# Plane copies without waits on their own buffer, a buffer choice by age, and a new order for attention plus a token-mixing MLP

## The chip, the cores and the metric

One core of one Trainium2 chip. The time is the device time of one execution in microseconds, as the median of three runs. Profiles and times are of the same program.

## The reference

The input x has 2048 rows of 512. It is normalised by row (`xn`), and the result is the sum of x, of full multi-head attention over `xn` (32 heads of 16), and of a two-layer perceptron that mixes over the 2048 rows.

```python
    def _A_ref(x, wqkv, wo):
        qkv = (x @ wqkv).reshape(B, S, 3, H, Dh) ...
        scores = jnp.einsum("bhqd,bhkd->bhqk", q, k) * scale
        p = _softmax(scores, axis=-1)
        o = jnp.einsum("bhqk,bhkd->bhqd", p, v)
        return o ... @ wo

    def _B_ref(x, w1, b1, w2, b2):
        h = _layernorm(x, axis=-1)
        u = _gelu(jnp.einsum("bsd,sf->bdf", h, w1) + b1)
        y = jnp.einsum("bdf,fs->bds", u, w2) + b2
        return y transposed

    xn = _layernorm(x, axis=-1)
    return x + _A_ref(xn, ...) + _B_ref(xn, ...)
```

The exponentials of the softmax are 32 x 2048 x 2048 values, by far the largest elementwise work.

## The kernel before

**Blocks and groups.** Attention is cut into 32 blocks: four query blocks of 512 rows times eight sets of four heads. A block has 16 groups, one for each tile of 128 keys, so there are 512 groups. In a group each of the four heads has a score tile of 128 keys by 512 queries; TensorE makes it with one matmul of 32 rows (`score_mm`, line 655) into a bank of PSUM.

**Two ways to the exponential.** A group belongs to ScalarE or to VectorE. ScalarE's way takes two score tiles at a time from two banks and writes both exponentials with one instruction (`exp_tile`, line 663, 128 x 1024), two instructions a group, from banks 0 to 3 in turn. VectorE's way builds the bits of the exponential by arithmetic on integers: `dve_first` (line 710) turns one score tile of 128 x 512 into 16-bit integers that are read as bf16, four such first copies a group; they fill a *plane* of 128 x 2048. `add_plane` (line 715) then makes two more planes from it by adding a shift, so that the sum of the three approximates the exponential. VectorE's scores go to banks 4, 5 and 7. Both ways end in TensorE's products with the values (`pv_mm`, line 675), gathered in bank 6: four matmuls for a ScalarE group, four for each plane of a VectorE group. The reciprocal of the softmax's sum and its product follow for each block on VectorE, through memory, and on GpSimd (POOL).

**Planes.** There are 19 places for planes. Two, in `plx`, serve nothing else. The others lie over tensors that are no longer needed at some time: four over `x_sb`, four over `xn_sb`, two each over `h_sb`, `w1blk` and `wqkv_sb`, three over `xnT`. The recording layer knows dependencies by keys, and `plane_alias` holds the keys of the tensor under a plane. `dve_first` and `add_plane` name them among what they write. `plane_take` takes the first free place of the list (`planes_avail`).

**Who decides the order.** Each operation is recorded by `Sched.add` (line 202) with its keys, an occupied interval and a latency. A planner in the kernel keeps a clock for each engine (`pe_step`, `dve_step`, chains of background work), picks the next operation for the engine that is free, and so writes the order of all five engines when the program is built. Which group goes to which engine follows from it as well: `d_take` and `d_fetch` hand a group to VectorE when one of its banks is free. The intervals of VectorE come from `T_DVE` (line 420). The planner's choices are steered by `POLICY`, one row of weights for each 10 us of its clock. `plan` (line 262) turns dependencies into semaphore waits. On the chip each engine runs its own list in that order and waits for semaphores only; TensorE in particular takes scores, value products and all other matmuls in the written order.

**Start and end.** The first four tiles of x are normalised, transposed, and give the first queries and keys, in an order written out by hand; scores begin after it. At the end `tail_epilogue` normalises the last block and adds four row tiles of the output: for the tiles in `HL` the rest of the sum is split in two bf16 parts by POOL and added by identity matmuls (`part_mm`), and ScalarE copies the bank; for the others VectorE adds it.

The two statements around which the change turns:

```python
                          reads=[("bank", bk)], writes=[("pl", pb, r)] + plane_alias[pb], name="p1", **T_DVE(512))
...
            pb = planes_avail()[0]
```

Of the kernel before, what the change touches and what calls it, by code (L numbers as in the profile page):

```python
# [15 lines left out]
D = 512  # L16
# [48 lines left out]
class Op:  # L65
# [26 lines left out]

SEG = 10000.0
POLICY = [
# [245 lines left out]
def bass_parallel_sum__softmax_full_mha__mixer_token_mlp__prompt_kernel(  # L340
# [18 lines left out]
    with ExitStack() as es:  # L359
# [60 lines left out]
        def T_DVE(n, div=1.0):  # L420
            return dict(occ=(n / div + 70.0) / 0.96, lat=(n / div + 70.0) / 0.96 + 135.0)
# [138 lines left out]
        def ln_norm(t):  # L560
            return sc.add("dve", lambda e: e.tensor_scalar(xn_sb[:, t, :], x_sb[:, t, :], mv[:, t, 0:1], mv[:, t, 2:3],
                                                           ALU.subtract, ALU.mult),
                          reads=[("x", t), ("mv", t), ("mvr", t)], writes=[("xn", t)], occ=300, lat=440, two=True)
# [17 lines left out]
        def ln2_norm(t):  # L581
            return sc.add("dve", lambda e: e.tensor_scalar(h_sb[:, t, :], xn_sb[:, t, :], r2[:, t:t + 1], None,
                                                           ALU.mult),
                          reads=[("xn", t), ("r2",)], writes=[("h", t)], occ=300, lat=440, two=True)
# [52 lines left out]
        def v_scale(t0_, n, T):  # L637
# [5 lines left out]
                          writes=[("V", 1, t0_ + i, T) for i in range(n)], two=True, **T_DVE(136 * n, 2.0))  # L643
# [63 lines left out]
        plane_i = [z.bitcast(I16) for z in plane_b]  # L707

        def dve_first(g, r, bk, pb):
            return sc.add("dve", lambda e: e.tensor_scalar(plane_i[pb][:, 512 * r:512 * (r + 1)], bank(bk), BIAS, 0.0,  # L710
                                                           ALU.add, ALU.max),
                          reads=[("bank", bk)], writes=[("pl", pb, r)] + plane_alias[pb], name="p1", **T_DVE(512))

        def add_plane(j, pb0, pb):
# [3 lines left out]
                          writes=[("pl", pb, r) for r in range(4)] + plane_alias[pb], name="plane", two=True, **T_DVE(2048, 4.0))  # L718
# [71 lines left out]
        xnT_evac(1, 1, 5, 0, "act")  # L790
        transpose_mm(2, 0, 0)
# [3 lines left out]
        k_mm(0, KB, 0)  # L795
        transpose_mm(3, 1, 0)
        xnT_evac(3, 1, 1, 0, "dve")
        k_evac(0, 1, KB, 0, "act")
        for t in range(3):
            qt0_mm(t, QB)  # L800
# [3 lines left out]
        k_mm(1, 3, 0)  # L804
        k_mm(2, 3, 1)
        k_mm(3, 3, 2)
# [3 lines left out]
        k_evac(1, 3, 3, 0)  # L810
# [16 lines left out]
        TOL, JOIN, DEFER, P1_PRI, D_PEND, FAR, D_HUNGRY, PACE, N_SAME, PRESS, PL_PRI, D_LAST, SEED = POLICY[0]  # L827
        kt_done = {0: 4}
        vt_done = {0: 4}
        k0_done = set(range(NPRE))  # L830
# [126 lines left out]
        def chain_ut(ft, due, rel):  # L957
# [15 lines left out]
            def u_evac():  # L973
# [3 lines left out]
                    reads=[("bank", xb), ("b1h",)], writes=[("gT", ft)], occ=650, lat=800)  # L977
# [1017 lines left out]
```

## Time and profile before

| | |
|---|---|
| median of three runs | 689.53 us (689.36 to 689.55) |
| profiled execution | 689.35 us, its span 687.1 us |
| granted TensorE clock | 1.00 |
| ScalarE (ACT) busy | 675.5 us, 98% |
| VectorE (DVE) busy | 660.6 us, 96% |
| TensorE (PE) busy | 649.8 us, 95% |
| GpSimd (POOL) busy | 68.3 us, 10% |
| moved from and to memory | 32.65 MB, 48 GB/s on average |

A row of a group reads: line of the kernel, engine, operation, what it writes and reads, shapes, how often; then busy time and the mean duration of one in ns; then the idle time of the engine just before these instructions and what ended it. A row of the timeline reads: start and duration in us, engine, line, operation, and how many equal instructions follow each other in it. `PEld` is TensorE's loading of weights, which overlaps its matmuls.

### The profile page before, as it was taken

To read this page: it belongs to the slowest core of one execution; us is meant where nothing else is said; L and a number is where in the kernel's file an instruction comes from. 1 tells how busy PE (TensorE), PEld (TensorE's weight loads), DVE (VectorE), ACT (ScalarE), POOL (GpSimd) and SP (SyncE) were. 2 spreads that over 40 slices of the span, in tenths; PEclk is the share of its full clock that TensorE was granted. 3 is DMA by queue.
4 is the path that set the end of the run, shared out by engine and by line. 5 is a ranking of instruction groups with operands and counts; after the bars stand their busy time and mean duration, and the time that the engine had idled before them with its cause. 6 is when DMAs were issued, how large, how long until landed. Compare 5 with 4: busy or idle time off the path is not lost.

```text
span 687.1 us, 15560 instructions
## 1 busy us (share of the span) xinstructions
PE 649.8 (95%) x6200; PEld 197.5 (29%) x6287; DVE 660.6 (96%) x1159; ACT 675.5 (98%) x737; POOL 68.3 (10%) x100
## 2 busy tenths in 40 slices
PE   8999999999999999999999999999998999999987
PEld 4433333322222222222222222222222222222222
DVE  7889999999999999999999999999999999999996
ACT  6999999999999999999999999999999999999996
POOL 6610100000000000000000001000000000001110
PEclk9999999999999999999999999999999999999999
DMA  7151100022212222210021211221120212212001
GB/s 215 32 100 26 34 26 4 28 49 46 63 40 53 49 59 48 43 29 18 21 53 48 53 43 43 54 52 37 43 55 23 60 47 62 57 46 62 14 22 46
DMA packets 78367, 32.65 MB, mean 48 GB/s; under 512 B 63004, under 2 KB 74204, under 8 KB 78296
## 3 DMA queue, kind: packets, MB, share of 16 engines
q1 hardware_dynamic: 77864, 31.27, 18.9%
q8 instruction: 49, 0.80, 0.5%
q10 hardware_dynamic: 432, 0.39, 0.2%
q14 instruction: 22, 0.18, 0.1%
HBM read 26.08 MB, written 2.61 MB: 42 GB/s over the span
## 4 chain that ended last, share of the span: by engine, by line
ACT 84%; PE 11%; DVE 3%; issue 1%; DMA 0%; POOL 0%; DVEq 0%
ACT pT L663 84%; PE ps L655 4%; PE ps L675 4%; PE ps L995 1%; DVE x_sb L710 1%; DVE plx L710 1%; PE ps L964 1%; DVE x_sb L715 1%; DVE plx L715 1%; PE ps L1712 0%; DMA x_sb<-in_A_x_dram 0%; PE ps L1005 0%; PE ps L1013 0%; DVE stats L527 0%; PE ps L596 0%
## 5 line engine op out<-in xcount | busy, mean ns | idle before, releaser
L663 ACT ACTIVATE pT<-ps 128x1024 bf16<-128x1024 f32 x720 | 661.0, 1128 | 0.7 <-PE ps L655 0.5
L655 PE MATMUL ps<-QT,KT 32*128 32x512 bf16 x2048 | 288.8, 384 | 23.1 <-ACT pT L663 18.6
L710 DVE TENSOR_SCALAR plx<-ps 128x512 int16<-128x512 f32 x344 | 225.0, 678 | 2.6 <-PE ps L655 1.6
L710 DVE TENSOR_SCALAR x_sb<-ps 128x512 int16<-128x512 f32 x244 | 166.1, 683 | 7.0 <-PE ps L655 0.8
L655 PEld LDWEIGHTS ps<-QT,KT 32*128 32x128 bf16 x2048 | 72.8, 91 | 271.2 <-ACT pT L663 254.5
L675 PE MATMUL ps<-pT,V 128*32 128x512 bf16 x1440 | 143.0, 390 | 0.7 <-DVE V L592 0.4
L715 DVE TENSOR_SCALAR x_sb<-plx 128x2048 int16<-128x2048 int16 x135 | 91.3, 683 | 0.3
L675 PEld LDWEIGHTS ps<-pT,V 128*32 128x32 bf16 x1440 | 36.9, 93 | 80.5 <-issue 73.8
L675 PE MATMUL ps<-plx,V 128*32 128x512 bf16 x592 | 56.9, 382 | 0.5 <-issue 0.5
L675 PE MATMUL ps<-x_sb,V 128*32 128x512 bf16 x592 | 56.3, 382 | 0.0
L1243 POOL TENSOR_TENSOR oT<-OT,denb 128x512 bf16<-128x512 f32 x16 | 20.3, 1270 | 316.0 <-DVE x_sb L715 210.9
L964 PE MATMUL ps<-h_sb,w1blk 128*128 128x512 bf16 (+1 forms) x153 | 49.4, 386 | 2.3 <-issue 2.2
L995 PE MATMUL ps<-gT,w2blk 128*128 128x512 bf16 (+1 forms) x149 | 48.3, 385 | 2.5 <-issue 2.4
L675 PE MATMUL ps<-x_sb,V17b 128*32 128x512 bf16 x484 | 47.5, 383 | 0.8 <-issue 0.3
L1243 POOL TENSOR_TENSOR otmp<-OT,denb 128x512 bf16<-128x512 f32 x15 | 19.1, 1272 | 262.6 <-DMA denb<-rec_scr 109.9
L715 DVE TENSOR_SCALAR x_sb<-x_sb 128x2048 int16<-128x2048 int16 x65 | 44.1, 682 | 0.4 <-PE ps L675 0.4
L715 DVE TENSOR_SCALAR plx<-x_sb 128x2048 int16<-128x2048 int16 x54 | 37.6, 696 | 0.3 <-PE ps L675 0.3
L596 PE MATMUL ps<-xnT,wqkv_sb 128*128 128x512 bf16 (+1 forms) x166 | 34.5, 305 | 2.1 <-issue 1.6
L1206 DVE COPY OT<-ps 128x512 f32<-128x512 f32 x31 | 21.1, 680 | 0.0
L596 PE MATMUL ps<-wqkv_sb,xnT 128*128 128x128 bf16 x256 | 20.9, 221 | 0.0
L995 PEld LDWEIGHTS ps<-gT,w2blk 128*128 128x128 bf16 (+1 forms) x176 | 12.4, 97 | 25.5 <-issue 22.1
L964 PEld LDWEIGHTS ps<-h_sb,w1blk 128*128 128x128 bf16 (+1 forms) x176 | 12.4, 99 | 25.3 <-issue 22.6
(96 smaller groups left out, 335.7 us busy)
## 6 DMA issues: line engine op xcount, KB each, us to landing
denb<-rec_scr SPq DMA_DIRECT2D x124, 64.0 KB, 2.2
w1blk<-in_B_w_dram SPq DMA_DIRECT2D x10, 512.0 KB
w2blk<-in_B_w_dram SPq DMA_DIRECT2D x16, 320.0 KB
xres<-in_A_x_dram SPq DMA_DIRECT2D x16, 128.0 KB, 2.1
QT<-qst SPq DMA_DIRECT2D x120, 16.0 KB, 1.8
out_dram<-osb SPq DMA_DIRECT2D x14, 128.0 KB, 1.7
wqkv_sb<-in_A_wqkv_dram SPq DMA_DIRECT2D x3, 384.0 KB, 8.3
x_sb<-in_A_x_dram SPq DMA_DIRECT2D x2, 512.0 KB
```

Source lines behind the costliest of these rows:

```text
L596: return sc.add("pe", lambda e: e.matmul(dst, lhsT=lhsT, rhs=rhs, start=(ct == 0), stop=(ct == NCT - 1)), reads=reads, writes=[("bank", bk ...
L655: return sc.add("pe", lambda e: e.matmul(bank(bk), lhsT=KT[32 * r:32 * r + 32, T, 128 * kt:128 * (kt + 1)], rhs=QT[32 * r:32 * r + 32, slo ...
L663: return sc.add("act", lambda e: e.activation(pT[:, buf, :], ps[:, slot * 1024:(slot + 1) * 1024], ACTF.Exp, scale=EXP_SCALE), reads=[("ba ...
L675: return sc.add("pe", lambda e: e.matmul(bank(PV_BANK)[32 * r:32 * r + 32, :], lhsT=vt_[:, off:off + 32], rhs=rhs, start=start, stop=stop, ...
L710: return sc.add("dve", lambda e: e.tensor_scalar(plane_i[pb][:, 512 * r:512 * (r + 1)], bank(bk), BIAS, 0.0, ALU.add, ALU.max), reads=[("b ...
L715: return sc.add("dve", lambda e: e.tensor_scalar(plane_i[pb], plane_i[pb0], float(SHIFT[j]), BITS_MAX, ALU.add, ALU.min), reads=[("pl", pb ...
L964: op = sc.add("pe", lambda e: e.matmul(bank(xb)[0:m, :], lhsT=w1blk[:, slot, st, 0:m], rhs=h_sb[:, st, :], start=(st == 0), stop=(st == NT ...
L995: op = sc.add("pe", lambda e: e.matmul(bank(xb), lhsT=w2blk[0:m, slot, ft, :], rhs=gT[0:m, ft, :], start=first, stop=last), reads=([("w2bl ...
L1206: op = sc.add("dve", lambda e: e.tensor_copy(OT32[:, eb, :], bank(PV_BANK)), reads=[("bank", PV_BANK)], writes=[("OT32", eb)], **T_DVE(512))
L1243: op = sc.add("pool", lambda e: e.tensor_tensor(dst, OT32[:, eb, :], denb[:, :], ALU.mult), reads=[("OT32", eb)] + [("denb", r) for r in r ...
```

## The change

It has six parts.

1. `dve_first` and `add_plane` write only the plane's own keys. The last operations on the tensor beneath are looked up once, when a place is first used (`plane_after`), and given as dependencies.
2. `plane_take` takes the free place whose last use ended first by the planner's clock (`plane_free`), in place of the first of the list.
3. Intervals and latencies of VectorE's operations are other numbers: `T_DVE`, both norms, the scaled copy of V, the bias copy, the reciprocal.
4. Keys of tiles 1 to 3 leave the hand-written start and become a chain (`chain_k1`) that the planner places; only tile 0 is there at first. The matmuls of the first queries move up between the transposes.
5. Two first copies of one group whose banks are neighbours may become one instruction (`dve_first2`), where the policy's new last number allows it.
6. `HL` loses the fourth tile, and all rows of `POLICY` are new, with one more number each.

```diff
 POLICY = [
-    (115.0, 80.0, 250.0, -1, 0, 1300.0, 0.0, 0.05, 2, 3, 2, 7500.0, 0),
-    (95.0, 50.0, 250.0, -1, 0, 2000.0, 0.0, 0.0, 3, 3, 2, 10500.0, 63069),
...
+    (115.0, 80.0, 250.0, -1, 0, 1300.0, 0.0, 0.05, 2, 3, 2, 7500.0, 0, 0.0),
+    (210.0, 40.0, 250.0, -1, 0, 900.0, 300.0, 0.05, 3, 2, 2, 7000.0, 0, 1.0),
...
         def T_DVE(n, div=1.0):
-            return dict(occ=(n / div + 70.0) / 0.96, lat=(n / div + 70.0) / 0.96 + 135.0)
+            return dict(occ=(n / div + 64.0) / 0.96, lat=(n / div + 64.0) / 0.96 + 141.0)
...
+        plane_old = {}
+        def plane_after(pb):
+            if pb not in plane_old:
+                z = set()
+                for k in plane_alias[pb]:
+                    z.update([sc.last_writer[k]] if k in sc.last_writer else [])
+                    z.update(sc.readers.get(k, ()))
+                plane_old[pb] = sorted(z, key=lambda o: (o.eng, o.pos))
+            return plane_old[pb]
...
-                          reads=[("bank", bk)], writes=[("pl", pb, r)] + plane_alias[pb], name="p1", **T_DVE(512))
+                          reads=[("bank", bk)], writes=[("pl", pb, r)], extra_deps=plane_after(pb), name="p1", **T_DVE(512))
+        def dve_first2(g, r, bk, r2_, bk2, pb):
+            dst = plane_i[pb].rearrange("p (r n) -> p r n", n=512)[:, r:r2_ + 1:r2_ - r, :]
+            src = ps.rearrange("p (b n) -> p b n", n=512)[:, bk:bk2 + 1:bk2 - bk, :]
+            return sc.add("dve", lambda e: e.tensor_scalar(dst, src, BIAS, 0.0, ALU.add, ALU.max),
+                          reads=[("bank", bk), ("bank", bk2)], writes=[("pl", pb, r), ("pl", pb, r2_)], extra_deps=plane_after(pb),
+                          name="p1", **T_DVE(1024))
...
-                          writes=[("pl", pb, r) for r in range(4)] + plane_alias[pb], name="plane", two=True, **T_DVE(2048, 4.0))
+                          writes=[("pl", pb, r) for r in range(4)], extra_deps=plane_after(pb), name="plane", two=True, **T_DVE(2048, 4.0))
...
         xnT_evac(1, 1, 5, 0, "act")
+        qt0_mm(0, QB)
+        k_mm(0, KB, 0)
         transpose_mm(2, 0, 0)
         ln_norm(3)
         v_ones(0)
         xnT_evac(2, 1, 0, 0, "dve")
-        k_mm(0, KB, 0)
+        qt0_mm(1, QB)
+        k_evac(0, 1, KB, 0, "act")
         transpose_mm(3, 1, 0)
         xnT_evac(3, 1, 1, 0, "dve")
-        k_evac(0, 1, KB, 0, "act")
-        for t in range(3):
-            qt0_mm(t, QB)
+        qt0_mm(2, QB)
         qt0_mm(3, 4)
         qt_evac(0, QB, "act", 0, 384)
         qt_evac(0, 4, "act", 384, 512, "QTh")
-        k_mm(1, 3, 0)
-        k_mm(2, 3, 1)
-        k_mm(3, 3, 2)
...
-        k_evac(1, 3, 3, 0)
...
-        k0_done = set(range(NPRE))
+        k0_done = {0}
...
-        HL = (0, 1, 3)
+        HL = (0, 1)
...
+        def chain_k1(due):
+            def kdone():
+                op = k_evac(1, 3, 5, 0)
+                k0_done.update((1, 2, 3))
+                return op
+            c = Chain("k1", [Step("pe", lambda t=t: k_mm(t, 5, t - 1), 226) for t in (1, 2, 3)]
+                      + [Step("dve", kdone, 470, frees=True)], due, -1.0, bk=[5])
+            c.banks = (5,)
+            return c
...
+        ex_queue.append(chain_k1(-2.0))
         ex_queue.append(chain_v0(-0.95))
...
+        def plane_free(pb):
+            t = sc.ready(writes=[("pl", pb, r) for r in range(4)])
+            return max([t] + [o.end for o in plane_after(pb)]) if pb not in plane_old else t
...
-            pb = planes_avail()[0]
+            pb = min(planes_avail(), key=plane_free)
...
+        def d_pairs(heads, banks):
+            banks = banks[:len(heads)]
+            if PAIR:
+                heads.sort(key=lambda h: (h[0]["g"], h[1]))
+                banks.sort()
+            return list(zip(heads, banks))
...
+                    for k2 in dbank:
+                        if PAIR and k2 == k + 1 and dbank[k2] is not None and dbank[k2][0] <= t + PAIR and dbank[k2][1] is dbank[k][1] \
+                                and dbank[k2][2] > dbank[k][2]:
+                            def p12(k=k, k2=k2):
...
+                                op = dve_first2(dg["g"], r, k, dbank[k2][2], k2, dg["pl"][0])
```

The other new intervals, in ns: norm 300 to 318, second norm 300 to 264, bias copy 650 to 658, reciprocal 175 to 186; the scaled copy of V is planned at four elements a cycle in place of two.

More of the change, by code (lines that the diff above doesn't have):

```diff
@@ L562, in ln_norm @@
                                                            ALU.subtract, ALU.mult),
-                          reads=[("x", t), ("mv", t), ("mvr", t)], writes=[("xn", t)], occ=300, lat=440, two=True)
+                          reads=[("x", t), ("mv", t), ("mvr", t)], writes=[("xn", t)], occ=318, lat=450, two=True)
         def ln2_rs(i):
@@ L583, in ln2_norm @@
                                                            ALU.mult),
-                          reads=[("xn", t), ("r2",)], writes=[("h", t)], occ=300, lat=440, two=True)
+                          reads=[("xn", t), ("r2",)], writes=[("h", t)], occ=264, lat=405, two=True)
         ps_bf = ps.bitcast(BF16)
@@ L642, in v_scale @@
                           reads=[("V", 0, t0_ + i, T) for i in range(n)] + [("Vone", t0_ // 4)],
-                          writes=[("V", 1, t0_ + i, T) for i in range(n)], two=True, **T_DVE(136 * n, 2.0))
+                          writes=[("V", 1, t0_ + i, T) for i in range(n)], two=True, **T_DVE(136 * n, 4.0))
         def blk_of(g):
@@ L826, in bass_parallel_sum__softmax_full_mha__mixer_token_mlp__prompt_kernel @@
         pv_open = [True]
-        TOL, JOIN, DEFER, P1_PRI, D_PEND, FAR, D_HUNGRY, PACE, N_SAME, PRESS, PL_PRI, D_LAST, SEED = POLICY[0]
+        TOL, JOIN, DEFER, P1_PRI, D_PEND, FAR, D_HUNGRY, PACE, N_SAME, PRESS, PL_PRI, D_LAST, SEED, PAIR = POLICY[0]
         kt_done = {0: 4}
         vt_done = {0: 4}
-        k0_done = set(range(NPRE))
+        k0_done = {0}
         v0_done = set()
@@ L976, in u_evac @@
                     gT[0:m, ft, :], bank(xb)[0:m, :], b1h[0:m, ft:ft + 1], None, ALU.add),
-                    reads=[("bank", xb), ("b1h",)], writes=[("gT", ft)], occ=650, lat=800)
+                    reads=[("bank", xb), ("b1h",)], writes=[("gT", ft)], occ=658, lat=800)
                 ut_done[0] += 1
@@ L1221, in rec @@
                 return sc.add("dve", lambda e: e.reciprocal(den_s[:, eb, :], den_s[:, eb, :]),
-                              reads=[("den_s", eb)], writes=[("den_s", eb)], occ=175, lat=330)
+                              reads=[("den_s", eb)], writes=[("den_s", eb)], occ=186, lat=330)
             def out1():
@@ L1663, in pe_step @@
                             frb.sort(key=lambda k: sc.ready(writes=[("bank", k)]))
-                            heads = list(zip(d_take(len(frb), p), frb))
+                            heads = d_pairs(d_take(len(frb), p), frb)
                         score_mm(g, p[0], 2 * slot, False)
@@ L1687, in pe_step @@
                 frb = [q for q in d_room() if sc.ready(writes=[("bank", q)]) <= t]
-                hs = list(zip(d_take(len(frb)), frb))
+                hs = d_pairs(d_take(len(frb)), frb)
                 if hs:
@@ L1782, in dve_step @@
                     c.append((P1_PRI if all(dbank[q] or ex_active[q] for q in dbank) else 1, dbank[k][0], p1))
+                    for k2 in dbank:
+                        if PAIR and k2 == k + 1 and dbank[k2] is not None and dbank[k2][0] <= t + PAIR and dbank[k2][1] is dbank[k][1] \
+                                and dbank[k2][2] > dbank[k][2]:
+                            def p12(k=k, k2=k2):
+                                _, dg, r = dbank[k]
+                                op = dve_first2(dg["g"], r, k, dbank[k2][2], k2, dg["pl"][0])
+                                dbank[k] = dbank[k2] = None
+                                dg["n1"] += 2
+                                dg["t"] = max(dg["t"], op.end)
+                                if dg["n1"] == 4:
+                                    pv_items[dg["g"] // NKT].append((dg["t"], "D", dg["g"], dg["pl"][0], 0))
+                            c.append((c[-1][0], c[-1][1] - 1e-3, p12))
             pool_on = sc.wide > t
@@ L1838, in bass_parallel_sum__softmax_full_mha__mixer_token_mlp__prompt_kernel @@
             while n_seg[0] * SEG <= t:
-                TOL, JOIN, DEFER, P1_PRI, D_PEND, FAR, D_HUNGRY, PACE, N_SAME, PRESS, PL_PRI, D_LAST, SEED = POLICY[min(n_seg[0], len(POLICY) - 1)]
+                TOL, JOIN, DEFER, P1_PRI, D_PEND, FAR, D_HUNGRY, PACE, N_SAME, PRESS, PL_PRI, D_LAST, SEED, PAIR = POLICY[min(n_seg[0], len(POLICY) - 1)]
                 n_seg[0] += 1
```

132 rows, old and new, of the table POLICY are left out of this document.

## The prediction

> **What bounds the kernel now.** I read the page first (busy shares, then the chain of waits), then the groups by line for ScalarE (ACT) and VectorE (DVE).
>
> ```profile
> span 687.1 us, 15560 instructions
> PE 649.8 (95%) x6200; PEld 197.5 (29%) x6287; DVE 660.6 (96%) x1159; ACT 675.5 (98%) x737; POOL 68.3 (10%) x100
> ACT 84%; PE 11%; DVE 3%; issue 1%; DMA 0%; POOL 0%; DVEq 0%
> ...
> L663 ACT ACTIVATE pT<-ps 128x1024 bf16<-128x1024 f32 x720 | 661.0, 1128 | 0.7 <-PE ps L655 0.5
> ...
> L710 DVE TENSOR_SCALAR plx<-ps 128x512 int16<-128x512 f32 x344 | 225.0, 678 | 2.6 <-PE ps L655 1.6
> L710 DVE TENSOR_SCALAR x_sb<-ps 128x512 int16<-128x512 f32 x244 | 166.1, 683 | 7.0 <-PE ps L655 0.8 <-PE ps L675 0.5
> ```
>
> ACT is on the chain for 84% of the span, and one line of it, the exponential, is 661.0 us in 720 instructions with 0.7 us of idle time before them all. 661.0 / 720 = 0.918 us is what one more or one less is worth (the mean of 1128 ns is longer, because neighbours overlap). The ACT rows in order of time give the rest of the skeleton:
>
> ```profile
> 9.08 1.57 ACT L616 ACTIVATE QT<-ps,qmask 128x384 bf16<-128x384 f32 x4 [0.68 <-PE ps L596]
> 10.52 20.38 ACT L663 ACTIVATE pT<-ps 128x1024 bf16<-128x1024 f32 x22
> ...
> 669.60 10.19 ACT L663 ACTIVATE pT<-ps 128x1024 bf16<-128x1024 f32 x11
> 682.51 1.09 ACT L590 ACTIVATE osb<-ps 128x512 bf16<-128x512 f32 x2 [2.72 <-PE ps L1013]
> 684.02 0.60 ACT L590 ACTIVATE xres<-ps 128x512 bf16<-128x512 f32 x1 [0.42 <-PE ps L1013]
> ```
>
> The first exponential starts at 10.52, the last ends at 669.60 + 10.19 = 679.79, and 7.3 us of closing work follow. So the time is 10.5 us of start, a full ACT, and 7.3 us of tail. The 96% of DVE matters too: it is the second engine that is nearly full, and what ACT no longer does has to be done there.
>
> **The change, term by term.** *Exponentials.* The policy table steers an order written when the program is built, so I counted the instructions of both built programs. Exponentials: 720 before, 714 after. Groups of four heads given to DVE: 152 before, 155 after. The sum has 6 x 0.918 = 5.5 us less on ACT. It is worth that only if scores arrive in time, which is DVE's side of the account.
>
> *DVE's new work.* Three groups are 12 more first copies (L710) and 6 more plane copies (L715). What does one occupy?
>
> ```profile
> 301.35 0.68 DVE L715 TENSOR_SCALAR x_sb<-plx 128x2048 int16<-128x2048 int16 x1
> 301.95 1.48 DVE L710 TENSOR_SCALAR x_sb<-ps 128x512 int16<-128x512 f32 x2
> ...
> 312.26 1.28 DVE L710 TENSOR_SCALAR x_sb<-ps 128x512 int16<-128x512 f32 x2
> ...
> 318.45 1.28 DVE L710 TENSOR_SCALAR plx<-ps 128x512 int16<-128x512 f32 x2
> 319.65 0.68 DVE L715 TENSOR_SCALAR x_sb<-x_sb 128x2048 int16<-128x2048 int16 x1
> 320.25 0.68 DVE L710 TENSOR_SCALAR plx<-ps 128x512 int16<-128x512 f32 x1
> ```
>
> Start to start it is 0.60 us for either kind (301.35 to 301.95, 319.65 to 320.25); the 0.68 contains the overlap with the next one. So 18 x 0.60 = 10.8 us more. Twelve of the copies are issued as six double ones over two banks. No row shows such an instruction; one lies between 0.60 (one copy) and 1.20 (two copies). I take 1.20, because its elements are those of two; the other end would give back 3.6 us.
>
> *The false waits.* Of the pairs above, the one at 301.95 takes 1.48 us, so its second copy starts 1.48 - 0.68 = 0.80 after the first; the two at 312.26 and 318.45 start 0.60 apart. In the DVE stream, 301.95 is two copies into one plane of x_sb, 312.26 two planes of x_sb, 318.45 one plane of plx. Only planes laid over another tensor (x_sb, xn_sb and others) carry that tensor's keys, and two writers of the same keys wait for each other; plx has none. The stream has 57 such neighbours in x_sb and 7 in xn_sb: 64 x 0.20 = 12.8 us of DVE time that the change frees. In the changed stream 153 neighbours fall on one aliased plane, none with such a wait.
>
> The Trainium skill speaks against this term: "VectorE: DVE Perf Modes", section "The DRAIN you can't avoid", has eight copies taking 13.88 us with a semaphore after each and with one after the last, so that the semaphore costs nothing. By it the change would free nothing here; the trace disagrees (0.80 against 0.60), and the measurement decides. What follows if the 0.20 is not the wait's is a rival below.
>
> *Does DVE keep up?* Busy time by stretch, columns PE, PEld, DVE, ACT, POOL:
>
> ```profile
> 36.00:200.00 164.00, 158.30 (x1550) 51.33 (x1573) 158.96 (x283) 163.46 (x179) 9.85 (x8) 1.00 0.20 43
> 200.00:330.00 130.00, 124.61 (x1180) 34.80 (x1194) 127.47 (x215) 129.86 (x142) 8.90 (x7) 1.00 0.18 40
> 330.00:500.00 170.00, 160.05 (x1497) 45.06 (x1519) 167.03 (x282) 169.98 (x183) 10.16 (x8) 1.00 0.18 45
> 500.00:670.00 170.00, 160.02 (x1552) 44.84 (x1569) 166.80 (x281) 170.00 (x187) 15.41 (x14) 1.00 0.18 45
> ```
>
> DVE's idle time from 36 to 670 us is 5.04 + 2.53 + 2.97 + 3.20 = 13.7 us. A false wait shows only 0.80 - 0.68 = 0.12 of its 0.20 as idle; the other 0.08 x 64 = 5.1 us are inside "busy". So DVE has 18.8 us above its bare work: 12.8 false waits and 6.0 other. The change asks 10.8 for new work and 5.5 because the span shrinks: 16.3, which leaves 2.5 us in that stretch. If all 6.0 us of other idle time are waits that DVE cannot shed, ACT is held for 6.0 - 2.5 = 3.5 us; if it is slack, for nothing. A second count goes along the two streams, from the first DVE copy to the last (each tied by its bank to the score and so to a number of exponentials): at 0.60 a copy, DVE lies 23 us below ACT's time before and about 5 after, and from the 200th exponential on the two run level. That is a close fit, with some room at its two ends, so I take +1.5 us, between 0 and 3.5.
>
> *Start.* Keys of tiles 1 to 3 now come after the first scores, and their copy to KT stands in the DVE stream behind four instructions that it used to precede:
>
> ```profile
> 8.75 0.68 DVE L527 BATCH_NORM_STATS2 stats<-x_sb 128x6 f32<-128x512 bf16 x1
> 9.46 0.18 DVE L531 BATCH_NORM_AGGREGATE mv<-stats 128x2 f32<-128x6 f32 x1
> 9.99 0.56 DVE L592 CAST KT<-ps 128x384 bf16<-128x384 f32 x1 [0.35 <-PE ps L596]
> 10.47 0.68 DVE L527 BATCH_NORM_STATS2 stats<-x_sb 128x6 f32<-128x512 bf16 x1
> 11.19 0.18 DVE L531 BATCH_NORM_AGGREGATE mv<-stats 128x2 f32<-128x6 f32 x1
> 11.29 0.38 DVE L561 TENSOR_SCALAR xn_sb<-x_sb,mv 128x512 bf16<-128x512 bf16 x1
> 11.58 0.69 DVE L527 BATCH_NORM_STATS2 stats<-x_sb 128x6 f32<-128x512 bf16 x1
> ...
> 8.21 1.75 PE L596 MATMUL ps<-xnT,wqkv_sb 128*128 128x128 bf16 x28
> 9.97 0.39 PE L655 MATMUL ps<-QT,KT 32*128 32x512 bf16 x2
> ```
>
> The first scores hang on the four QT copies of ACT, which start when the third tile of QT is through, so the 12 key matmuls taken from behind it (12 of the 28, 12/28 x 1.75 = 0.75 us of PE) free nothing: the first exponential stays at about 10.5. But only one key tile is there, which feeds two exponentials. Without the copy at 9.99 the four instructions move up by its 10.47 - 9.99 = 0.48, the last ending at 11.58 + 0.69 - 0.48 = 11.8; then the copy (0.56) and the scores, which lead their exponential by 10.52 - 9.97 = 0.55: about 12.9 for the third, where an unbroken ACT would want it at 10.52 + 2 x 0.918 = 12.36. I take +0.5, between 0 (the copy finds an earlier place) and 1.0 (all moves are late as well).
>
> *Tail.* The fourth row tile of the end goes through DVE, not ACT, and two identity matmuls and two POOL splits vanish.
>
> ```profile
> 682.52 0.38 PE L1005 MATMUL ps<-wo_c,oT 128*128 128x512 bf16 x1
> 682.74 0.59 PE L1043 MATMUL ps<-gT,ident 128*128 128x512 bf16 x2
> 683.17 0.38 PE L1013 MATMUL ps<-wo_pad,oT 128*128 128x512 bf16 x1
> 683.39 0.59 PE L1013 MATMUL ps<-wo_pad,otmp 128*128 128x512 bf16 x2
> 683.80 0.69 DVE L1905 TENSOR_TENSOR xres<-ps,h_sb 128x512 bf16<-128x512 f32 x1 [1.45 <-PE ps L1013]
> ```
>
> The four matmuls ahead of 683.39 are gone or stand before the wait for otmp, so those at 683.39 can start at 682.52, 0.87 earlier. DVE then adds the third tile at 682.93 and the fourth 0.60 later, ending at 684.22; ACT's copy of it ended at 684.02 + 0.60 = 684.62. So -0.4 (0 if the order before them costs it). The store behind keeps its length.
>
> *At nothing:* the corrected intervals and "longest free first" emit no instruction; they act through the counts above. Three more groups on DVE mean nine more PE batches of plane products and three fewer of pT; PE's weight loads before scores idle mostly for ACT, so six batches are hidden there.
>
> **Sum.** The profiled execution took 689.35, 2.25 more than its span and 0.18 less than the median of 689.53. 689.35 - 5.5 + 1.5 + 0.5 - 0.4 = 685.45; with the 0.18, 685.6.
>
> **Rivals.** (1) *DVE keeps up wholly and the start closes its hole:* 689.53 - 5.5 - 0.4 = 683.6. For it: ACT lost only 0.7 us so far; against: DVE's room fell to 2.5 us. (2) *DVE becomes the bound, and it is slower than before.* Place: from the 200th exponential on, where the two run level. First copies wait for their scores (plx, which has no false waits, idled 2.6 us over 344 copies, 8 ns each). Each wait that the tighter order adds now goes to the end. Break-even is where DVE's unshed time is above what it has by what the change gains: 2.5 us of room plus 5.5 - 0.1 of gain, 7.9 us, or 13 ns for each of 620 copies over today's idle share; at 25 ns, 15.5 - 2.5 = 13.0, and 689.53 - 5.4 + 13.0 = 697.1. Against: the 0.60 us grid holds through the quoted rows. (3) *The 0.20 us is not the wait's.* Then 153 neighbours cost 0.20 each, 30.6 us against the 2.5 us of room, so 28.1 on the path: 689.53 - 5.4 + 28.1 = 712. The row at 312.26 speaks against it: same tensor, no wait, 0.60. This is what the Trainium skill's rule would come to. (4) *The planner's order does not deliver:* ACT loses in many small gaps what six exponentials give: 688.2 to 690.9, no change.
>
> **How the numbers follow.** What a measurement of this kernel can tell from no change is about 0.2%, 1.4 us. Chances: forecast, with its own range 684.4 to 688.0, 0.63; (1) 0.19; (4) 0.08; (2) 0.08; (3) 0.02. Faster 0.82, same 0.08, slower 0.10. The range: low, rival (1) with 0.3 us of it for the double copies, 683.3; high, +3.5 for DVE and +1.0 for the start with no gain in the tail, 689.53 - 5.5 + 4.5 = 688.5.
>
> **What would show it.** Right: 714 exponentials at 0.918 each; neighbours in one plane 0.60 apart and no pair at 0.80; DVE idle under 6 us between 36 and 670; the third exponential about 0.5 us late; last ACT copies two, with two DVE additions behind each other. Wrong: more than 3 us of idle time before the exponentials, with scores held by DVE (rival 2), or pairs still 0.80 apart (rival 3).

## The result, and the profile after

| | before | after |
|---|---|---|
| median | 689.46 us (689.36 to 689.55, 4 runs) | 684.00 us (683.83 to 684.57, 4 runs) |
| profiled execution, its span | 689.35, 687.1 | 684.02, 682.2 |
| exponentials on ACT | 720 | 714 |

The ratio (of the means) is 0.9922, with an interval of 0.9905 to 0.9939: 5.5 us less, where 3.9 us were forecast. The measured 684.0 lies inside the whole range of the prediction (683.3 to 688.5), but outside the narrower range of its forecast (684.4 to 688.0), on the side of the first rival. In the runs below, those with a mean granted clock of 0.991 to 0.993 (two of `e4`, two of `e5`, one of `e9`) came 3 to 4 us above the other runs of their kernel, which hardly moves a median but moves a ratio. First the page of the changed kernel: busy shares, the chain that ended last, and the groups that answer to those of before.

```profile
span 682.2 us, 15375 instructions
PE 645.9 (95%) x6217; PEld 196.9 (29%) x6304; DVE 663.2 (97%) x1172; ACT 669.7 (98%) x730; POOL 66.6 (10%) x98
...
ACT 85%; PE 10%; DVE 3%; POOL 1%; issue 0%; DVEq 0%
...
L664 ACT ACTIVATE pT<-ps 128x1024 bf16<-128x1024 f32 x714 | 655.9, 1135 | 1.1 <-PE ps L656 0.9
...
L722 DVE TENSOR_SCALAR x_sb<-ps 128x512 int16<-128x512 f32 x184 | 120.3, 678 | 0.4
L722 DVE TENSOR_SCALAR xn_sb<-ps 128x512 int16<-128x512 f32 x132 | 86.9, 679 | 2.6 <-PE ps L656 2.2
...
L722 DVE TENSOR_SCALAR plx<-ps 128x512 int16<-128x512 f32 x86 | 56.3, 678 | 0.4 <-PE ps L656 0.4
```

ACT still makes up 85% of the chain, so it still sets the end. Its exponentials are busy for 655.9 us in place of 661.0. Their idle time went from 0.7 to 1.1 us. DVE's copies into `x_sb` lost their idle time (7.0 us for 244 before, 0.4 us for 184 now), though by the built programs 153 neighbours of DVE's list, and no longer 64, now write one aliased plane.

Next the timeline of ACT (start and duration in us; in brackets the idle time before and what ended it).

```profile
9.16 1.57 ACT L617 ACTIVATE QT<-ps,qmask 128x384 bf16<-128x384 f32 x4 [0.86 <-PE ps L597]
10.60 1.95 ACT L664 ACTIVATE pT<-ps 128x1024 bf16<-128x1024 f32 x2
13.18 30.39 ACT L664 ACTIVATE pT<-ps 128x1024 bf16<-128x1024 f32 x33 [0.63 <-PE ps L656]
43.84 18.64 ACT L664 ACTIVATE pT<-ps 128x1024 bf16<-128x1024 f32 x20 [0.28 <-PE ps L656]
...
662.98 12.18 ACT L664 ACTIVATE pT<-ps 128x1024 bf16<-128x1024 f32 x13
678.01 1.08 ACT L591 ACTIVATE osb<-ps 128x512 bf16<-128x512 f32 x2 [2.86 <-PE ps L1030]
```

The first exponential starts at 10.60 (10.52 before), the third after a hole of 0.63. The last one ends at 662.98 + 12.18 = 675.16 (679.79 before), and 682.2 - 675.16 = 7.04 us follow (7.31 before). So the span of 4.9 us less is made of: exponentials -5.1, idle time before them +0.4, first start +0.1, tail -0.3. What lies outside the span was 1.8 us against 2.2.

The 36th exponential starts at 43.84, after 2 + 33 others. In the kernel before it is this one:

```profile
42.82 1.03 ACT L663 ACTIVATE pT<-ps 128x1024 bf16<-128x1024 f32 x1
```

So by then the changed kernel is 1.0 us behind. Its idle time shows 0.63 + 0.28 = 0.9 of it, the first start 0.1. From there to the end of the last exponential it takes 675.16 - 43.84 = 631.3 us for 679, the kernel before 679.79 - 42.82 = 637.0 us for 685. That is 0.930 us each in both.

The timeline of DVE shows the pieces that were forecast from other rows:

```profile
12.15 0.54 DVE L593 CAST KT<-ps 128x384 bf16<-128x384 f32 x1
...
162.58 1.22 DVE L730 TENSOR_SCALAR xnT<-ps 128x1024 int16<-128x1024 f32 x1
163.72 0.68 DVE L735 TENSOR_SCALAR xn_sb<-x_sb 128x2048 int16<-128x2048 int16 x1
...
663.05 2.47 DVE L722 TENSOR_SCALAR wqkv_sb<-ps 128x512 int16<-128x512 f32 x4
...
671.06 0.69 DVE L735 TENSOR_SCALAR x_sb<-plx 128x2048 int16<-128x2048 int16 x1
675.78 0.78 DVE L1927 STREAM_TRANSPOSE denb<-ps 128x256 f32<-128x256 f32 x2 [4.04 <-PE ps L676]
...
678.45 1.29 DVE L1957 TENSOR_TENSOR xres<-ps,h_sb 128x512 bf16<-128x512 f32 x2 [0.59 <-PE ps L1030]
```

The key copy comes at 12.15 and makes the hole. A double copy takes 163.72 - 162.58 = 1.14 us start to start. Four copies into one aliased plane take 2.47 us, that is (2.47 - 0.68) / 3 = 0.60 each, with no wait left between them. DVE is through with its last plane at 671.06 + 0.69 = 671.75, 3.4 us before the last exponential ends. In the kernel before, the same view shows how close that was:

```profile
678.36 0.69 DVE L715 TENSOR_SCALAR x_sb<-plx 128x2048 int16<-128x2048 int16 x1
680.28 0.78 DVE L1875 STREAM_TRANSPOSE denb<-ps 128x256 f32<-128x256 f32 x2 [1.23 <-PE ps L675]
```

There the last plane ended at 679.05, 0.7 us ahead of ACT. So DVE, with three more groups to do, stands 2.7 us further ahead at the end. Busy time by stretch, columns as in the table of before (PE, PEld, DVE, ACT, POOL, granted clock, share of DMA, GB/s):

```profile
36.00:200.00 164.00, 158.73 (x1575) 51.41 (x1592) 159.82 (x288) 163.71 (x180) 9.84 (x8) 1.00 0.20 43
200.00:330.00 130.00, 126.19 (x1206) 35.62 (x1208) 129.84 (x219) 129.92 (x143) 8.66 (x7) 1.00 0.18 41
330.00:500.00 170.00, 160.09 (x1524) 44.98 (x1547) 169.64 (x289) 169.96 (x182) 10.41 (x9) 1.00 0.19 47
500.00:670.00 170.00, 160.48 (x1555) 45.20 (x1575) 169.11 (x287) 169.96 (x186) 13.68 (x12) 1.00 0.18 44
```

DVE's idle time from 36 to 670 us is 4.18 + 0.16 + 0.36 + 0.89 = 5.6 us, from 13.7. From 200 us on it is 1.4 us in 470: both engines are full.

### The profile page after: what moved, and what is told of

Its sections match the earlier page's. It is cut to its first block, busy times and chain, and to the rows that moved or that the text cites. A ratio compares the mean times of both kernels' runs of the same rounds, so it can differ in the third digit from the quotient of the medians.

```text
span 682.2 us, 15375 instructions
## 1 busy us (share of the span) xinstructions
PE 645.9 (95%) x6217; PEld 196.9 (29%) x6304; DVE 663.2 (97%) x1172; ACT 669.7 (98%) x730; POOL 66.6 (10%) x98
## 4 chain that ended last, share of the span: by engine, by line
ACT 85%; PE 10%; DVE 3%; POOL 1%; issue 0%; DVEq 0%
ACT pT L664 84%; PE ps L656 4%; PE ps L676 3%; PE ps L597 1%; PE ps L1012 1%; ACT gT L1003 1%; PE ps L794 1%; DVE stats L528 0%; PE ps L981 0%; POOL r L579 0%; PE ps L749 0%; DVE h_sb L583 0%; DVE xnT L593 0%; DVE xn_sb L562 0%; DVE KT L593 0%
## 5 line engine op out<-in xcount | busy, mean ns | idle before, releaser
L664 ACT ACTIVATE pT<-ps 128x1024 bf16<-128x1024 f32 x714 | 655.9, 1135 | 1.1 <-PE ps L656 0.9
L722 DVE TENSOR_SCALAR x_sb<-ps 128x512 int16<-128x512 f32 x184 | 120.3, 678 | 0.4
L722 DVE TENSOR_SCALAR xn_sb<-ps 128x512 int16<-128x512 f32 x132 | 86.9, 679 | 2.6 <-PE ps L656 2.2
L722 DVE TENSOR_SCALAR plx<-ps 128x512 int16<-128x512 f32 x86 | 56.3, 678 | 0.4 <-PE ps L656 0.4
L722 DVE TENSOR_SCALAR xnT<-ps 128x512 int16<-128x512 f32 x66 | 43.2, 679 | 0.0
L722 DVE TENSOR_SCALAR wqkv_sb<-ps 128x512 int16<-128x512 f32 x56 | 36.7, 679 | 0.2
L676 PE MATMUL ps<-x_sb,V 128*32 128x512 bf16 x344 | 33.3, 381 | 0.0
L676 PE MATMUL ps<-xn_sb,V 128*32 128x512 bf16 x296 | 28.9, 381 | 0.0
L722 DVE TENSOR_SCALAR h_sb<-ps 128x512 int16<-128x512 f32 x44 | 28.8, 679 | 0.0
L722 DVE TENSOR_SCALAR w1blk<-ps 128x512 int16<-128x512 f32 x40 | 26.4, 677 | 0.0
L735 DVE TENSOR_SCALAR xn_sb<-x_sb 128x2048 int16<-128x2048 int16 x31 | 20.9, 680 | 0.0
```

What stands on the lines that cost most here:

```text
L664: return sc.add("act", lambda e: e.activation(pT[:, buf, :], ps[:, slot * 1024:(slot + 1) * 1024], ACTF.Exp, scale=EXP_SCALE), reads=[("ba ...
L676: return sc.add("pe", lambda e: e.matmul(bank(PV_BANK)[32 * r:32 * r + 32, :], lhsT=vt_[:, off:off + 32], rhs=rhs, start=start, stop=stop, ...
L735: return sc.add("dve", lambda e: e.tensor_scalar(plane_i[pb], plane_i[pb0], float(SHIFT[j]), BITS_MAX, ALU.add, ALU.min), reads=[("pl", pb ...
```

## The experiments

In all kernels but two (`e7` and `e8`, which the planner orders anew) the order of every engine's instructions is that of the kernel they start from, apart from what their diff adds or swaps. So a difference comes from the one edit, not from another plan. Each kernel is compared with runs of the kernel before that were made beside it on the same chip: 689.64 us for `e1` to `e4`, 689.84 for `e5` to `e8`, 689.69 for `e9` to `e11`, which ran on another chip. "Dose" means small fills of a scratch tile put into DVE's list; they compute nothing that is used.

### Waits alone

**`e1_before_nowait`**: the kernel before, in its own order, without the waits between two writers of an aliased plane. The planner's clock still sees them; the program doesn't.

```diff
+        own = set()
         for k in writes:
             w = self.last_writer.get(k)
             if w is not None:
-                deps.add(w)
+                if name in ("p1", "plane") and k[0] != "pl" and w.name in ("p1", "plane"):
+                    own.add(w)
+                else:
+                    deps.add(w)
...
-        for d in op.deps:
+        for d in op.deps + list(own):
             t = max(t, d.end)
```

> The kernel before, every engine's order as it was, only the waits between two copies into one aliased plane buffer left out. My account (ACT sets the end, the false waits cost DVE room and not time): 689.4, within 0.5 us of the kernel before, neighbours in one x_sb plane 0.60 us apart in place of 0.80, DVE's idle time between 36 and 670 us up from 13.7 by nothing or more. Rival a (the waits were on the path, so that their removal alone is the gain): 689.5 - 5.5 = 684. Rival b (the 0.20 us belongs to the place and not to the wait): 689.4 and neighbours still 0.80 apart.

Measured: 688.88 us in 12 runs, ratio 0.9988 (0.9979 to 0.9997): 0.8 us less. DVE's timeline, the group of exponentials and the sum of the four stretches from 36 to 670 us:

```profile
301.18 1.28 DVE L714 TENSOR_SCALAR x_sb<-ps 128x512 int16<-128x512 f32 x2
```

```profile
L667 ACT ACTIVATE pT<-ps 128x1024 bf16<-128x1024 f32 x720 | 660.9, 1131 | 0.1
```

```profile
sum 634.00, PE 619.45 PEld 175.66 DVE 619.97 ACT 633.87 POOL 44.43; mean PE 154.86 PEld 43.91 DVE 154.99 ACT 158.47 POOL 11.11
```

The neighbours in `x_sb` of which the prediction showed 1.48 now take 1.28, so they are 0.60 apart, and the 0.20 us was the wait's. In the whole trace 57 pairs of successive copies into `x_sb` or `xn_sb` start 0.77 to 0.82 apart in the kernel before, and 3 in `e1`. But DVE's idle time stays at 634.0 - 620.0 = 14.0 us (13.7 before): the time that 64 waits had taken is now spent waiting for TensorE, for scores above all: 5.9 us of the idle time end with them, from 2.4. ACT's idle time before exponentials fell from 0.7 to 0.1, about what the end moved. The waits filled room; they hardly set the time.

**`e2_after_waits`**: the changed kernel, in its order, with the waits put back between successive writers of one aliased plane.

```diff
+        def same(pb, op):
+            if plane_alias[pb]:
+                if pb in plane_last:
+                    same_buf.append((op, plane_last[pb]))
+                plane_last[pb] = op
+            return op
...
+        for op, d in same_buf:
+            op.deps.append(d)
         sc.plan()
```

> The changed kernel, every engine's order as it is, with the waits between two writers of one aliased plane buffer put back. My account: 153 neighbouring copies at 0.80 us in place of 0.60 cost DVE 30.6 us; its room in this order is some 3 to 6 us, so the time is 684.0 + 25 to 28 = 709 to 712. Rival a (a wait on the engine's own last instruction costs nothing): 684.0. Rival b (half of them fall where DVE would wait for scores anyway): 684.0 + 10 to 15 = 694 to 699.

Measured: 712.71 us in 4 runs, ratio 1.0331 (1.0315 to 1.0348), just above the 709 to 712 that were expected. The changed kernel took 683.89 beside it, so this one is 28.8 us longer. From its page the span, the clock in 40 slices, the chain and the exponentials:

```profile
span 710.7 us, 15834 instructions
...
PEclk9999999999999999999799999999999999999999
...
PE 56%; DVE 33%; issue 5%; ACT 5%; POOL 1%; DMA 0%; DVEq 0%
...
L664 ACT ACTIVATE pT<-ps 128x1024 bf16<-128x1024 f32 x714 | 670.4, 1046 | 15.0 <-PE ps L656 10.1
```

From DVE's timeline:

```profile
299.94 1.48 DVE L730 TENSOR_SCALAR xnT<-ps 128x512 int16<-128x512 f32 x2
301.33 0.68 DVE L743 TENSOR_SCALAR x_sb<-xn_sb 128x2048 int16<-128x2048 int16 x1
301.93 1.48 DVE L730 TENSOR_SCALAR xnT<-ps 128x512 int16<-128x512 f32 x2
```

Pairs are 1.48 - 0.68 = 0.80 us apart again: in the whole trace 145 of successive copies into one aliased tensor are 0.77 to 0.82 apart, against 3 in the changed kernel. ACT's share of the chain falls from 85% to 5%: DVE is late with the banks, TensorE waits in its written order, and ACT behind it. A wait for the instruction just before, on the same engine, is not free here: 153 neighbours at 0.20 are 30.6 us, and the end is 28.8 us later. Not all of that need be the waits'. The granted clock fell to 0.7 in one slice, and its mean was 0.992 to 0.995 in the four runs, where the four runs of the changed kernel in the table above had 0.999 or 1.000. What share the slower clock had was not separated. An estimate from the runs at 0.991 to 0.993 of other kernels is 3 to 4 us, which would leave about 25 for the waits. It may be more here, since TensorE stands on more of this chain.

**`e3_after_again`** is the changed kernel, run beside `e1`, `e2` and `e4`.

> The changed kernel once more, beside the others on the same chip: 684.0 within 0.6 us, span 682, 714 exponentials, first at 10.6, third at 13.2.

Measured: 683.89 us in 6 runs, ratio 0.9914 (0.9900 to 0.9928).

### The hole at the start

**`e4_after_key_copy_first`**: one swap in DVE's list, the key copy of tiles 1 to 3 ahead of the row statistics that stand before it.

```diff
+        ds = sc.streams["dve"]
+        i = ds.index(k1_op[0])
+        late = ds[i - 1]
+        ds[i - 1], ds[i] = ds[i], ds[i - 1]
```

> The changed kernel with one swap on DVE: the copy of the keys of tiles 1 to 3 goes ahead of the row statistics that stand before it. The statistics took 0.59 us start to start. My account: the third exponential comes 0.5 to 0.6 us earlier (12.6 in place of 13.18), ACT is unbroken after it, and the whole run ends 0.5 us earlier: 683.5. Rival (DVE runs level with ACT, so what ACT gains at the start it gives back at the first place where DVE is late): third exponential at 12.6 but the end unchanged, 684.0, with 0.5 us more idle time before the exponentials later on.

Measured: 684.21 us in 6 runs, ratio 0.9932 (0.9912 to 0.9953): no gain. ACT's timeline of `e4`, then that of `e3`:

```profile
10.50 3.94 ACT L664 ACTIVATE pT<-ps 128x1024 bf16<-128x1024 f32 x4
14.67 28.86 ACT L664 ACTIVATE pT<-ps 128x1024 bf16<-128x1024 f32 x31 [0.23 <-PE ps L656]
43.82 16.79 ACT L664 ACTIVATE pT<-ps 128x1024 bf16<-128x1024 f32 x18 [0.29 <-PE ps L656]
```

```profile
10.48 1.95 ACT L664 ACTIVATE pT<-ps 128x1024 bf16<-128x1024 f32 x2
13.07 30.44 ACT L664 ACTIVATE pT<-ps 128x1024 bf16<-128x1024 f32 x33 [0.64 <-PE ps L656]
43.80 16.80 ACT L664 ACTIVATE pT<-ps 128x1024 bf16<-128x1024 f32 x18 [0.28 <-PE ps L656]
```

The swap does close the hole: the third exponential follows the second without a break. Yet both kernels have done 35 exponentials at 43.8 us. By the single starts in the two traces, `e4` is 0.58 us ahead of `e3` at the third exponential, 0.23 at the fifth, and 0.02 behind from the tenth on. The row at 14.67 is the fifth, which waits. What stands before it in `e4` (`PEld` is TensorE's loading of weights):

```profile
13.12 0.40 DVE L562 TENSOR_SCALAR xn_sb<-x_sb,mv 128x512 bf16<-128x512 bf16 x1
...
13.58 0.23 PEld L749 LDWEIGHTS ps<-ident,xn_sb 128*128 128x128 bf16 x4 [0.32 <-DVE xn_sb L562]
...
14.24 0.39 PE L656 MATMUL ps<-QT,KT 32*128 32x512 bf16 x2
```

The same normalisation in `e3`:

```profile
13.11 0.40 DVE L562 TENSOR_SCALAR xn_sb<-x_sb,mv 128x512 bf16<-128x512 bf16 x1
```

DVE normalises a later tile, TensorE waits for it with that tile's transposes (L749), and the fifth exponential's scores (14.24) stand behind them in TensorE's order. DVE's work of the start is the same in both kernels, so this normalisation comes at the same time in both, with or without the hole. That it holds the fifth exponential in `e4` is read from these rows. For the 0.23 us that go between the fifth and the tenth it is argued by likeness, and no run took the normalisation away. That the hole itself doesn't set the time is shown.

### How much room DVE has

**`e5_after_dose`** and **`e6_before_nowait_dose`**: 60 fills, spread over DVE's list from the 130th first copy to the 600th, in the changed kernel and in `e1`.

```diff
+        pad = sb("pad", [128, 128], F32)
+        p1s = [o for o in sc.streams["dve"] if o.name == "p1"]
+        for i in range(60):
+            at = p1s[130 + (600 - 130) * i // 60]
+            x_ = Op("dve", lambda e: e.memset(pad[:], 0.0), "pad")
+            sc.streams["dve"].insert(sc.streams["dve"].index(at) + 1, x_)
```

> The changed kernel, every engine's order as it is, with 60 small fills of a scratch tile (128 x 128 f32, estimated at 0.15 us each, 9 us together) spread over DVE's stream between its 130th and 600th first copy. Account from e4 (DVE runs level with ACT, no room): the time rises by nearly all of it, 683.9 + 7 to 9 = 691 to 693. The prediction's account (2.5 us of room in that stretch): 683.9 + 6.5 = 690.4. Rival (ACT alone sets the end): 683.9.

> The kernel before without the false waits, order as it was, with the same 60 fills. DVE has 13.7 us of visible idle time there, so my account is no change to the same kernel without fills: 688.9, at most +0.7. Rival (the order of 720 exponentials is as tight on DVE as that of 714): 688.9 + 7 to 9 = 697.

Measured: `e5` 685.50 us in 10 runs, ratio 0.9945 (0.9928 to 0.9961), 1.6 more than the changed kernel (2.1 by the two ratios, which go by means); `e6` 689.20 in 10 runs, ratio 0.9995 (0.9985 to 1.0005), 0.3 more than `e1`. DVE's timeline of `e5` gives the true dose:

```profile
306.29 0.68 DVE L722 TENSOR_SCALAR x_sb<-ps 128x512 int16<-128x512 f32 x1
306.94 0.17 DVE L1997 MEMSET pad<- 128x128 f32 x1
307.03 0.62 DVE L722 TENSOR_SCALAR x_sb<-ps 128x512 int16<-128x512 f32 x1
307.57 0.67 DVE L735 TENSOR_SCALAR xn_sb<-xn_sb 128x2048 int16<-128x2048 int16 x1
```

Two copies and a fill take 307.57 - 306.29 = 1.28 us where two copies take 1.20. A fill of 0.17 us thus costs only 0.08, and the dose is 60 x 0.08 = 4.8 us, about half of what the expectation reckoned. Both accounts in it (690.4, and 691 to 693) were too high; with the true dose, the prediction's 2.5 us of room would give 686.2. Of 4.8 us, 1.6 to 2.1 reach the end and about 3 are swallowed. DVE's share of the chain rises to 62%, ACT's falls to 19%:

```profile
DVE 62%; ACT 19%; PE 15%; issue 1%; DMA 1%; POOL 1%; SPq 1%; DVEq 0%
```

So the changed kernel has some 3 us of room on DVE and no more. The order of before, once its waits are out, takes the same dose for 0.3 us.

**`e9_after_big_dose`**, **`e10_before_big_dose`**, **`e11_before_nowait_big_dose`**: 180 fills over the same stretch of the list (14.4 us by the 0.08 above), in the changed kernel, in the kernel before with its waits, and in `e1` without them. Each fill follows the one before by a wait as well.

```diff
+        for i in range(180):
+            at = p1s[130 + (600 - 130) * i // 180]
+            x_ = Op("dve", lambda e: e.memset(pad[:], 0.0), "pad")
+            x_.deps = [last_pad] if i else []
+            last_pad = x_
```

> The changed kernel, order as it is, with 180 of the small fills between DVE's 130th and 600th first copy. In e5 a fill made the distance of its neighbours 1.28 us in place of 1.20, 0.08 net, so 60 of them were 4.8 us, and the time rose by 1.6: 3.2 us of room. My account: 180 x 0.08 = 14.4 us, less 3.2: 683.9 + 11.2 = 695.1, between 694 and 696.5. Rival (the fills fall mostly into gaps that no account has seen; the rise goes on at a third of the dose): 688.7.

> The kernel before, with its false waits, order as it was, and the same 180 fills. The prediction's account: of its 18.8 us above bare work 12.8 are false waits, which stay, so 6.0 us of room: 689.6 + 14.4 - 6.0 = 698.0, between 696 and 700. Rival (a false wait's 0.20 us can be filled by a fill that comes to stand in it, so the waits are no loss of room): 689.6 to 691.

> The kernel before without the false waits, order as it was, and the same 180 fills. The prediction's account: 18.8 us of room, more than 14.4: 689.2, at most +1.5. Rival (the waits' time was no room that other work can use): the same as with the waits, 696 to 700.

The two values of `e1` and `e3` come from the first chip.

| | without fills | with 180 fills | more | ratio to before |
|---|---|---|---|---|
| changed kernel (`e3`, `e9`) | 683.89 | 694.15 | 10.3 | 1.0077 (1.0049 to 1.0105) |
| kernel before (`e10`) | 689.69 | 697.34 | 7.7 | 1.0112 (1.0097 to 1.0127) |
| the same without waits (`e1`, `e11`) | 688.88 | 690.61 | 1.7 | 1.0016 (1.0006 to 1.0025) |

The chain of `e9`, then of `e10`, then of `e11`:

```profile
DVE 66%; ACT 18%; PE 13%; issue 1%; POOL 1%; DVEq 0%
```

```profile
ACT 40%; PE 31%; DVE 25%; issue 3%; POOL 0%; DMA 0%; DVEq 0%
```

```profile
ACT 69%; DVE 17%; PE 12%; issue 1%; SPq 1%; DMA 1%; POOL 0%
```

Rows two and three are the same order under the same fills, and differ by the waits only: 697.34 - 690.61 = 6.7 us. The rival, that a fill can stand in a wait at no cost, holds for a few of them: 24 fills of `e10` fell between two copies into one aliased tensor, and 20 of these pairs are 0.78 to 0.80 apart, as they are without a fill. That makes its dose some 1.6 us smaller, so the 6.7 us are rather too little. So the waits' time, which was worth 0.8 us by itself (`e1`), is room that other work can use. `e11` rose by 1.7 us, so in that order too the room is used up at some places before the whole 14.4 us are in: DVE has 17% of its chain. `e9` gives the room of the changed kernel a second time, 14.4 - 10.3 = 4.1 us.

### Code and policy apart

**`e7_after_old_policy`**: all code of the change, with the rows of `POLICY` of before and no double copies. **`e8_before_new_policy`**: the code of before with the new rows, without their last number. The first two rows of the one and of the other:

```diff
 POLICY = [
     (115.0, 80.0, 250.0, -1, 0, 1300.0, 0.0, 0.05, 2, 3, 2, 7500.0, 0, 0.0),
-    (210.0, 40.0, 250.0, -1, 0, 900.0, 300.0, 0.05, 3, 2, 2, 7000.0, 0, 1.0),
+    (95.0, 50.0, 250.0, -1, 0, 2000.0, 0.0, 0.0, 3, 3, 2, 10500.0, 63069, 0.0),
```

```diff
 POLICY = [
     (115.0, 80.0, 250.0, -1, 0, 1300.0, 0.0, 0.05, 2, 3, 2, 7500.0, 0),
-    (95.0, 50.0, 250.0, -1, 0, 2000.0, 0.0, 0.0, 3, 3, 2, 10500.0, 63069),
+    (210.0, 40.0, 250.0, -1, 0, 900.0, 300.0, 0.05, 3, 2, 2, 7000.0, 0),
```

> All code of the change with the policy rows of before (last number 0, so no double copies): the planner writes a new order, and it holds 720 exponentials and 152 DVE groups again. By the number of exponentials: 689.0, with 0.5 to either side for start and tail. Rival (the code, not the rows, brings the gain): 684 to 685.

> The code of before with the policy rows of the change (without their last number): 730 exponentials and 147 DVE groups. By the number of exponentials: 689.5 + 10 x 0.918 = 698.6. Rival (the rows are better for any code): 684 to 689.

Measured: `e7` 690.38 us in 10 runs, ratio 1.0008 (0.9998 to 1.0017); `e8` 699.36 in 4 runs, ratio 1.0136 (1.0121 to 1.0151). The groups of exponentials of `e7` and of `e8`:

```profile
L664 ACT ACTIVATE pT<-ps 128x1024 bf16<-128x1024 f32 x720 | 661.3, 1134 | 1.0 <-PE ps L656 0.8
```

```profile
L663 ACT ACTIVATE pT<-ps 128x1024 bf16<-128x1024 f32 x730 | 670.8, 1139 | 1.0 <-PE ps L655 0.8
```

The code alone leaves the count at 720 and gives nothing: `e7` is 0.5 us above the kernel before, where 689.0 was expected. It has the new start too, and its 36th exponential starts at 43.84, 1.0 us late as in the changed kernel. The rows alone give 730 and lose 10 us. Together they give 714. In all three the time follows the count at about 0.92 us each, within 1 us and with 1.0 to 1.1 us of idle time: the new rows win beside the new code and lose beside the old. Which of the code's other parts (the choice of plane, the intervals) the rows need to come to 714 was not tried on the chip, and stays open.

## Why the prediction was right, and where its size was off

*What sets the end.* Right. ACT is 85% of the chain as it was 84%, and the plans with 714, 720 and 730 exponentials end in the order of their counts (`e7`, `e8`).

*Six exponentials, -5.5.* Right: 679 against 685 from the 36th on, at the same 0.930 us each with all that lies between them, and 655.9 / 714 = 0.919 of busy time each. Busy time fell by 5.1 only; the last section tells what busy time hides.

*The false waits, 12.8 us of room.* Right in kind, and the step on which the rest stands. The 0.20 us is the wait's (`e1`, `e2`), it is worth little by itself (0.8 us), and it is usable (6.7 us under the same dose). The rival by which the 0.20 is not the wait's would have `e2` at the time of the changed kernel; it came 28.8 us later, of which the clock may have a few. By "VectorE: DVE Perf Modes", section "The DRAIN you can't avoid", in the Trainium skill, which has a measurement of eight copies, a semaphore after each costs nothing extra. The trace does not agree with that for neighbouring copies on this kernel's DVE.

*DVE keeping up, +1.5.* This is the term that was mis-sized most, and it measured about 0. The working asked whether 6.0 us of DVE's other idle time were waits that it could not shed, took a value between 0 and 3.5, and the truth was the lower end. From the 36th exponential on, six fewer at 0.93 us would give 5.6 us, and 5.7 were measured: nothing was lost there. In `e1` DVE's idle time did not shrink when its waits went, so DVE had been ahead of what it waits for: slack, which more work fills. The account itself held. It left 2.5 us of room. The two doses measured 3 to 4, and the end of DVE's list lies 2.7 us further ahead of ACT's than before.

*Start, +0.5.* Right in place, and half of what was measured: the third exponential comes at 13.18, forecast 12.9, and the 36th 1.0 us later than before, the upper end of the range that was given (0 to 1.0). What failed in it is the cause: the sum named the key copy and let the delay end with it. `e4` takes that hole away and is as late by the tenth exponential: behind the copy stands DVE's normalisation of later tiles, for which TensorE waits with its transposes ahead of the scores.

*Double copies.* Six, at 1.14 us, where 1.20 was taken, between 0.60 and 1.20. Worth 0.4 us of DVE's room.

*Tail, -0.4.* -0.3; two additions of DVE behind each other as forecast, in 1.29 us.

*The total.* The profiled execution came out 5.3 us shorter, where the terms gave 3.9. Term by term: exponentials and DVE together -5.7, where -5.5 and +1.5 were reckoned, start 1.0 for 0.5, tail -0.3 for -0.4, and 0.4 less outside the span, which no term spoke of. So DVE's 1.5 us is the largest part of the error, and the start's 0.5 went the other way. The first rival (DVE keeps up wholly, 683.6) came nearer than the forecast, but with some luck: its other half, that the start closes its hole, did not happen, and the 0.4 us outside the span made up for part of that.

*Slower.* The rival by which DVE becomes the bound was not met, and how far it lay is known only roughly. The prediction put break-even at 7.9 us more on DVE. By the doses it is some 9 us, an estimate from 3 to 4 us of room and 5.5 of gain. `e5` (4.8 us more on DVE) already turns the chain to DVE, and `e9` (14.4) makes the changed kernel slower than the one before.

## What to carry to other kernels

A wait inside one engine that isn't the bound can cost room and hardly any time: taking it out pays when the work is dealt out anew. Here the freed room alone gave 0.8 us, the new rows alone lost 10, the new code alone gave nothing, and the whole change won 5.5. How much room an engine has is measured by a dose: a few dozen small instructions put into its list at fixed order, with the true cost of one read from the starts of its neighbours. Where an order is planned by weights, count the instructions of the bound engine in the built program before anything else; here it told the time of three plans within 1 us, from the one before (714, 720 and 730 against 720, at 0.92 us each).

## What was not expected of the hardware

The busy time of ACT hides lateness. Mean duration of an exponential is 1135 ns in the changed kernel at 0.919 us apiece, and 1046 in `e2`, where each comes later; there 15.0 us of idle time show, but busy time has grown by 14.5 us as well (670.4 against 655.9). So, of the 28.8 us that `e2` is longer, only half stands in the column of idle time. An instruction that overlaps its neighbour by up to 0.2 us can come that much later and no idle time appears. Read from the starts, the loss is whole. The smallest distance of two exponentials' starts is 0.904 us, which two thirds of the neighbours keep. What the others lie above it adds up to 10.3 us in the kernel before, 11.0 in the changed kernel and 39.7 in `e2`; 39.7 - 11.0 = 28.7 is nearly all of the 28.8. The idle column shows 0.7, 1.1 and 15.0. So in either kernel some 10 us lie between ACT and a list without a break, of which its idle time shows a tenth or less; how much of that could be won was not tried. DVE has the same on a smaller scale: a copy lasts 0.68 and follows the last by 0.60, and a fill of 0.17 us between two copies costs 0.08.
